# Seven quadrant products for the first mlp's upper projections in the third and fourth batch

## The chip, the cores and the metric

One core of a Trainium2 chip runs the whole program as one launch. The metric is the device time of that launch in microseconds (us); lower is better. The engines are TensorE (PE in the profile; PEld is its weight load), VectorE (DVE), ScalarE (ACT), GpSimd (POOL) and SyncE (SP), which issues most DMAs.

## The reference

Local attention over 4 batches, 8 heads, 576 positions and a head size of 64 gives x with 2304 tokens and 512 features. A first mlp follows: three upper projections from 512 to 768 features, the largest of the three, and a projection back to 512. A second mlp with 8 experts of 1024 hidden features, weighted by gates that are normalised in 8 rounds, gives the output. All numbers are float32.

```python
attn = softmax(mask(q @ k.T / 8)) @ v                      # window of 32, plain or with a step of 4
h = np.maximum(np.maximum(x @ w1, x @ w2), x @ w3)         # first mlp: 512 -> 768, three times
x2 = h @ w_out                                             # 768 -> 512
out = sum(P[:, e:e + 1] * (np.maximum(x2 @ v1[e], 0) @ v2[e]) for e in range(8))
```

## The kernel before

**Precision.** A float32 operand is held as a rounded high part and a low part (its remainder). `split` (L66 to L69) makes both: a copy on ACT for the high part, then a subtraction on POOL or DVE for the low part. A product of two operands takes three matmuls, high by high, high by low and low by high (`PASS`).

**Stages.** The first mlp runs batch by batch in the order of `WORK`: for batch b the six pieces `b.0` to `b.5` (128 hidden features each) through `up`, and then `b.out` through `down`, which projects back to 512 features, stores x2 and feeds the gates. Batch 0 and batch 1 share their last two pieces' weights, so `1.4` and `1.5` stand beside `0.4` and `0.5`. After batch 3 the second mlp begins with its stages (L802 and L756), in which seven products of quadrants already take the place of eight.

**Up.** For each piece, `up` takes the two halves of 288 tokens, and for each half the three projections. A projection is 12 matmuls (4 slices of the 512 features by 3 passes) of 128x128 weights and 288 columns (L377) into one of four PSUM banks of the pool `ps_g`. The first result is copied out by ACT (L383), the second and third are taken into the maximum by DVE (L385), and the last is split by ACT and DVE. The weights of a batch come from `wm1f` in DRAM by `load_w1`, 512 KB for two weight tiles, and are split again by ACT and POOL in every batch.

**Units and hooks.** PE runs in the order in which the program is written; the other engines' orders are made by a planner that simulates the program and prefers what was written earlier among what it takes to be ready. `up` counts a unit after each projection (12 matmuls), `down` after each 288-column result. After each unit `hooks` adds the attention of the next batch by the lists `BEGIN` and `STAGES`: scores and softmax at a head pair's first unit, the transposes 8 and 9 units later, the product with v and the write of x's high and low part (L256, L260) 11 units later. Batch 2's attention begins in batch 0 and runs beside batch 1; batch 3's runs beside batch 2; beside batch 3 there is none. In batches 1 to 3 a softmax is nine ACT instructions with a sum each (L200).

**Early.** Before the last `down`, `early` fetches the first two weight stages and the first 768 tokens of the second mlp, makes the sums T1 to T4 of x2's quadrants on DVE (L598) and splits them into tiles of the pool `xs`, which takes the place of batch 2's x (`xta`) from piece `3.0` on. The planner is free to run it as soon as its data and buffers are there.

**Buffers.** `raw` has 4 tiles, `wa` 8, `cx` 3 (x2 of a batch, the tokens and sums of `early`, and some others). A tile that is asked for takes any buffer that is free by then.

## Time and profile before

| what | value |
|---|---|
| time, median of 3 runs | 1901.99 us (1899.49 to 1902.62) |
| the profiled execution's own time | 1905.52 us |
| its span | 1903.7 us |
| mean granted TensorE clock | 0.99 |
| PE busy / DVE / ACT / POOL | 98% / 68% / 51% / 35% |
| DMA | 435 MB, 229 GB/s over the span |

The page gives busy time, the chain of work that ended last, and groups of instructions. A stretch of the span can be asked for by itself: batch 1 from `1.0` runs from 175.8 to 247.1 us (its `down` from 224), batch 2 from 247.1 to 342.3 us (its `down` from 317.1), batch 3 from 342.3 to 422.5 us (its `down` from 401.8), each bound read off PE's timeline.

### The profile page before, as it was taken

To read this page: it belongs to the slowest core of one execution; us is meant where nothing else is said; L and a number is where in the kernel's file an instruction comes from. 1 tells how busy PE (TensorE), PEld (TensorE's weight loads), DVE (VectorE), ACT (ScalarE), POOL (GpSimd) and SP (SyncE) were. 2 spreads that over 40 slices of the span, in tenths; PEclk is the share of its full clock that TensorE was granted. 3 is DMA by queue.
4 is the path that set the end of the run, shared out by engine and by line. 5 is a ranking of instruction groups with operands and counts; after the bars stand their busy time and mean duration, and the time that the engine had idled before them with its cause. 6 is when DMAs were issued, how large, how long until landed. Compare 5 with 4: busy or idle time off the path is not lost.

```text
span 1903.7 us, 33958 instructions
## 1 busy us (share of the span) xinstructions
PE 1858.2 (98%) x12105; PEld 1751.4 (92%) x12105; DVE 1295.0 (68%) x2454; ACT 966.6 (51%) x2337; POOL 667.2 (35%) x568
## 2 busy tenths in 40 slices
PE   7899999999999999999999999999999999999998
PEld 6799999998899987999899999999989999999997
DVE  7983333437866677666677777777777677876777
ACT  5663544324554444444456454565545554555544
POOL 2123433435666667666612121121211121221211
PEclk7899999999999999999999999999999999999999
DMA  7744444346667668666986766767798676776763
GB/s 257 269 154 168 154 145 166 131 171 232 230 249 260 254 252 307 250 252 257 347 282 223 239 217 226 247 224 237 228 333 265 213 233 225 228 255 212 233 221 100
DMA packets 206537, 435.23 MB, mean 229 GB/s; under 512 B 18848, under 2 KB 97312, under 8 KB 204832
## 3 DMA queue, kind: packets, MB, share of 16 engines
q1 hardware_dynamic: 203680, 429.12, 65.6%
q10 hardware_dynamic: 2688, 3.93, 0.7%
q8 instruction: 96, 1.57, 0.3%
q14 instruction: 73, 0.60, 0.1%
HBM read 313.97 MB, written 119.01 MB: 227 GB/s over the span
## 4 chain that ended last, share of the span: by engine, by line
PE 84%; DVE 8%; DMA 4%; issue 2%; ACT 2%; POOL 1%; SPq 0%; DVEq 0%; ACTq 0%; POOLq 0%
PE po L1011 25%; PE po L1106 12%; PE ps L377 10%; PE po L756 10%; PE p L1106 6%; PE q L1106 6%; PE q L802 4%; PE p L802 4%; PE ps L397 3%; DMA raw<-in_wm 1%; DVE sums L534 1%; DVE h L854 1%; DMA cx<-in_wm 1%; DVE ts L573 1%; DMA qt<-in_q 1%
## 5 line engine op out<-in xcount | busy, mean ns | idle before, releaser
L1011 PE MATMUL po<-wt,hop 128*128 128x256 f32 (+1 forms) x3264 | 482.9, 310 | 2.5 <-DVE r L987 2.5
L1011 PEld LDWEIGHTS po<-wt,hop 128*128 128x128 f32 x3264 | 445.0, 191 | 38.2 <-ACT hop L68 2.7
L69 POOL TENSOR_TENSOR wt<-raw,wt 128x256 fp32r<-128x256 f32 x192 | 186.4, 996 | 757.9 <-ACT wt L68 757.5
L69 DVE TENSOR_TENSOR hop<-r,hop 128x384 fp32r<-128x384 f32 x384 | 208.5, 572 | 190.2 <-ACT hop L68 185.1
L756 PE MATMUL po<-wb,h 128*128 128x512 f32 x1152 | 295.1, 392 | 0.4 <-POOL wb L69 0.4
L377 PE MATMUL ps<-xt,wa 128*128 128x288 f32 x1728 | 244.1, 299 | 5.6 <-DVE wa L290 2.0
L756 PEld LDWEIGHTS po<-wb,h 128*128 128x128 f32 x1152 | 213.5, 188 | 34.2 <-POOL wb L69 1.1
L377 PEld LDWEIGHTS ps<-xt,wa 128*128 128x128 f32 x1728 | 233.6, 190 | 9.6 <-DVE wa L290 2.3
L68 ACT CAST hop<-r 128x384 fp32r<-128x384 f32 x384 | 188.7, 516 | 56.7 <-DVE r L987 30.5
L69 POOL TENSOR_TENSOR wa<-raw,wa 128x512 fp32r<-128x512 f32 x112 | 135.9, 1217 | 89.6 <-ACT wa L68 87.7
L1120 ACT ACTIVATE r<-r 128x384 f32<-128x384 f32 x192 | 99.7, 525 | 127.6 <-DVE r L1119 126.7
L1106 PE MATMUL po<-xT,wa 128*128 128x384 f32 x768 | 155.9, 338 | 0.0
L1106 PEld LDWEIGHTS po<-xT,wa 128*128 128x128 f32 x768 | 136.6, 188 | 0.0
L69 POOL TENSOR_TENSOR tw<-ts,tw 128x512 fp32r<-128x512 f32 x64 | 85.3, 1355 | 93.4 <-DVE h L854 53.7
L1106 PE MATMUL po<-xB,wa 128*128 128x384 f32 x576 | 117.0, 338 | 0.0
L1040 DVE SCALAR_TENSOR_TENSOR acc<-po,prob,acc 128x256 f32<-128x256 f32 x222 | 95.0, 475 | 21.7 <-PE po L1011 17.6
L69 POOL TENSOR_TENSOR wa<-sums,wa 128x512 fp32r<-128x512 f32 x64 | 88.7, 1406 | 55.6 <-ACT wa L68 36.7
L1106 PEld LDWEIGHTS po<-xB,wa 128*128 128x128 f32 x576 | 102.4, 188 | 0.3 <-issue 0.3
L69 POOL TENSOR_TENSOR wb<-raw,wb 128x512 fp32r<-128x512 f32 x64 | 93.0, 1453 | 24.4 <-ACT wb L68 23.9
L981 DVE TENSOR_TENSOR r<-r,r 128x384 f32<-128x384 f32 x128 | 93.1, 727 | 2.2
L1022 ACT COPY mm<-po 128x256 f32<-128x256 f32 x144 | 49.6, 376 | 79.7 <-PE po L1011 79.7
L68 ACT CAST wa<-raw 128x512 fp32r<-128x512 f32 x112 | 61.6, 555 | 56.0 <-DMA raw<-in_wm 29.3
(183 smaller groups left out, 3106.6 us busy)
## 6 DMA issues: line engine op xcount, KB each, us to landing
wa<-wsd SPq DMA_DIRECT2D x192, 512.0 KB, 4.4
wt<-wtd SPq DMA_DIRECT2D x256, 256.0 KB, 3.6
wsd<-wa SPq DMA_DIRECT2D x96, 512.0 KB, 3.4
raw<-in_wm SPq DMA_DIRECT2D x64, 512.0 KB, 4.2
wtd<-tw SPq DMA_DIRECT2D x128, 256.0 KB, 2.8
raw<-in_wm SPq DMA_DIRECT2D x128, 256.0 KB, 5.4
wa<-wsd SPq DMA_DIRECT2D x64, 256.0 KB, 4.5
cx<-in_wm SPq DMA_DIRECT2D x12, 1024.0 KB, 6.9
```

The source lines that it names most:

```text
L68: nc.scalar.copy(hi, src)
L69: sub.tensor_tensor(out=lo, in0=src, in1=hi.bitcast(F32), op=ALU.subtract)
L377: nc.tensor.matmul(ps, w[:, wi, kk], xt[:, xi, kk, n0:n0 + HB], start=(n == 0), stop=(n == 3 * KT - 1),)
L397: nc.tensor.matmul(ps, wo[f][:, wi, d2 * P:(d2 + 1) * P], hs[f][:, hi, a * HB:(a + 1) * HB], start=(f == 0 and n == 0), stop=(f == NF1 - 1 ...
L756: nc.tensor.matmul(po, self.hs[f, j][:, hi, t * P:(t + 1) * P], self.ws[f][:, wi], start=(n + f + k == 0), stop=(n == NPAIR - 1 and f == 1 ...
L802: nc.tensor.matmul(ps, wo[w][:, wi, kk], xo[x][:, xi, kk], start=(first and k == 0), stop=True if k == 5 else False, skip_group_check=not ...
L981: nc.vector.tensor_tensor(out=r[o, n], in0=r[x, n], in1=r[y, n], op=op)
L1011: nc.tensor.matmul(self.ps[side, t][:, 0:x.shape[-1]], h[:, hi, t * P:(t + 1) * P], x, start=(first and i == 0), stop=(n == NPAIR - 1 and ...
L1022: nc.scalar.copy(m, self.ps[ORD[k][0], t][:, 0:256])
L1040: nc.vector.scalar_tensor_tensor(out=a, in0=src, scalar=g, in1=a, op0=ALU.mult, op1=ALU.add)
L1106: nc.tensor.matmul(ps[k][side], wo[k][w][:, wi, kk], xo[x][:, xi, kk], start=(first and c == 0), stop=c == 5, skip_group_check=not first,)
L1120: nc.scalar.activation(out=r, in_=r, func=AF.Relu)
```

## The change

In batches 2 and 3 `up` is replaced by `up_quads`. It takes two pieces at once (256 hidden features) and both halves of the tokens, cuts the weights into quadrants A11 to A22 and x into B11 to B22, and makes the four result quadrants from seven products of quadrants (A11 B11, A12 B21, S2 T2, S1 T1, S3 T3, S4 B22, A22 T4) instead of eight. A product is 6 matmuls of the same shape (2 slices by 3 passes), so a projection of two pieces takes 42 matmuls where it took 48. S2, S3 and A22 add onto the bank `p` of A11 after it has been copied out, S4 onto the bank `q` of S1.

- The weight sums S1 to S4 are made once: nine calls of `sums_w1`, three units apart from unit 58 on (pieces `1.0` to `1.out`), each with two loads, four DVE operations, two splits by ACT and POOL, and two stores of 512 KB into a new DRAM tensor `wsf`. `load_quads` loads them in batches 2 and 3, one projection ahead, beside A11, A12 and A22, which it splits as before.
- Attention's result for batches 2 and 3 is copied whole (`whole`, into a `cx` tile) instead of being split. `quads_first` and `quads_rest` make T1 to T4 on DVE and split all seven operands with ACT and DVE, at units 72 and 85 for batch 2 and 124 and 128 for batch 3.
- The running maximum of a projection over w1, w2, w3 is kept in a `cx` tile, `best`, which lives as long as `up_quads` of its batch. Three of the four results need an addition on DVE before the maximum.
- The two x buffers (`spaces`) now stay allocated to the end. T1, T2 and T3 of the second mlp lie in the first of them, and are loaded in two DMAs each instead of one.

A unit of `up_quads` ends after A12, S1, S4 and A22, so that a batch still has 36 units in `up`, and `BEGIN` is unchanged. The diff, shortened:

```diff
 BEGIN = {1: (0, 5, 10, 16), 2: (43, 60, 67, 73), 3: (92, 100, 108, 116)}
+SUMS = 58
+QUAD = {2: (72, 85), 3: (124, 128)}
...
+SPACE = 2 * KT * S
+QUADS = (("B11", "B21", "T2", "T1"), ("T3", "B22", "T4"))
...
-    xts = {}
+    xts, xf, spaces = {}, {}, [xta_p.tile([P, SPACE], F32R, name="xt")]
...
-        if p == 0:
-            xts[b] = (xtb_p if b % 2 else xta_p).tile([P, 2, KT, S], F32R, name="xt")
-        xt = xts[b]
+        if p == 0 and b < 2:
+            xts[b] = spaces[b].rearrange("p (s k n) -> p s k n", s=2, k=KT)
+        xt = xts.get(b)
...
+        def whole(a):
+            if b not in xf:
+                xf[b] = cx_p.tile([P, KT, S], F32, name="xf", tag="cx")
+            t0, t1 = halves[a]
+            for s0, s1, dst in pieces(t0 * QT, t1 * QT, dil):
+                nc.scalar.copy(dst(xf[b][:, p]), h["o", a][:, s0 - t0 * QT:s1 - t0 * QT])
...
-            ops[f"V{a}"], ops[f"H{a}"], ops[f"L{a}"] = partial(v, a), partial(hi, a), partial(lo, a)
+            ops[f"V{a}"] = partial(v, a)
+            ops[f"H{a}"], ops[f"L{a}"] = (partial(hi, a), partial(lo, a)) if b < 2 else (partial(whole, a), list)
...
+    wsf = dram.tile([3 * NF1 // 2, 2, P, 2, 512], F32, name="wsf")
+    def sums_w1(i):
+        raw = raw_p.tile([P, 2, 512], F32, name="raw")
+        for j in range(2):
+            g = 3 * (2 * (i // 3) + j) + i % 3
+            nc.sync.dma_start(raw[:, j], wm1f[g // 2, :, g % 2])
+        a11, a12, a21, a22 = (raw[:, j, c:c + 256] for j in range(2) for c in (0, 256))
+        for o, x, y, op in (
+            (a22, a21, a22, ALU.add), (a21, a11, a21, ALU.subtract),
+            (a11, a22, a11, ALU.subtract), (a12, a12, a11, ALU.subtract),
+        ):
+            nc.vector.tensor_tensor(out=o, in0=x, in1=y, op=op)
+        for j in range(2):
+            t = wa_p.tile([P, 2, 512], F32R, name="wa")
+            split(nc, t[:, 0], t[:, 1], raw[:, j], nc.gpsimd)
+            nc.sync.dma_start(wsf[i, j], t.bitcast(F32))
+    quads_w, best = {}, {}
+    def load_quads(b, i):
+        if i == 3 * NF1 // 2:
+            return
+        raw = raw_p.tile([P, 2, 512], F32, name="raw")
+        for j, c in ((0, 0), (1, 256)):
+            g = 3 * (2 * (i // 3) + j) + i % 3
+            nc.sync.dma_start(raw[:, j, c:512], wm1f[g // 2, :, g % 2, c:512])
+        a, x, y, z = (wa_p.tile([P, 2, 512], F32R, name="wa") for _ in range(4))
+        split(nc, a[:, 0], a[:, 1], raw[:, 0], nc.gpsimd)
+        nc.sync.dma_start(x.bitcast(F32), wsf[i, 0])
+        nc.sync.dma_start(y.bitcast(F32), wsf[i, 1])
+        split(nc, z[:, 0, 0:256], z[:, 1, 0:256], raw[:, 1, 256:512], nc.gpsimd)
+        quads_w[b, i] = {
+            name: t[:, :, c:c + 256].rearrange("p s (k m) -> p s k m", k=2)
+            for name, t, c in (
+                ("A11", a, 0), ("A12", a, 256), ("S2", x, 0), ("S4", x, 256),
+                ("S3", y, 0), ("S1", y, 256), ("A22", z, 0),
+            )
+        }
+    quads_x = {}
+    def quad(name):
+        k = int(name not in QUADS[0])
+        n = 4 * HB
+        i = QUADS[k].index(name) * n
+        return spaces[k][:, i:i + n].rearrange("p (s k n) -> p s k n", s=2, k=2)
+    def quads_first(b):
+        x = xf[b]
+        b11, b12 = x[:, 0:2, 0:HB], x[:, 0:2, HB:S]
+        src = {"B11": b11, "T1": b11}
+        for name in src:
+            if name == "T1":
+                nc.vector.tensor_tensor(out=b11, in0=b12, in1=b11, op=ALU.subtract)
+            t = quads_x[b, name] = quad(name)
+            split(nc, t[:, 0], t[:, 1], src[name], nc.vector)
+    def quads_rest(b):
+        x = xf.pop(b)
+        b11, b12, b21, b22 = (x[:, k:k + 2, n:n + HB] for k in (0, 2) for n in (0, HB))
+        for name, o, y, z in (
+            ("B21", b21, None, None), ("T2", b11, b22, b11), ("T3", b12, b22, b12),
+            ("B22", b22, None, None), ("T4", b21, b21, b11),
+        ):
+            if y is not None:
+                nc.vector.tensor_tensor(out=o, in0=y, in1=z, op=ALU.subtract)
+            t = quads_x[b, name] = quad(name)
+            split(nc, t[:, 0], t[:, 1], o, nc.vector)
+    def up_quads(b, f, unit):
+        h = [h1_p.tile([P, 2, S], F32R, name="h1") for _ in range(2)]
+        inner[b][f], inner[b][f + 1] = h
+        if f == 0:
+            best[b] = cx_p.tile([P, 2, 2, HB], F32, name="best", tag="cx")
+        for m in range(3):
+            i = 3 * f // 2 + m
+            load_quads(b, i + 1)
+            ws = quads_w.pop((b, i))
+            m1, u2, m5 = (at2_p.tile([P, HB], F32, name="tmp", bufs=3) for _ in range(3))
+            def bank():
+                return ps_g.tile([P, 512], F32, name="ps")[:, :HB]
+            def product(ps, w, x, first):
+                x = quads_x[b, x]
+                n = 0
+                for kk in range(2):
+                    for wi, xi in PASS:
+                        nc.tensor.matmul(
+                            ps, ws[w][:, wi, kk], x[:, xi, kk], start=(first and n == 0),
+                            stop=n == 5, skip_group_check=not first,
+                        )
+                        n += 1
+            def result(j, a, ps, c):
+                hi, lo = (h[j][:, s, a * HB:(a + 1) * HB] for s in range(2))
+                t = best[b][:, j, a]
+                if m == 0:
+                    if c is None:
+                        nc.scalar.copy(t, ps)
+                    else:
+                        nc.vector.tensor_tensor(out=t, in0=ps, in1=c, op=ALU.add)
+                    return
+                if c is None:
+                    c = ps
+                else:
+                    nc.vector.tensor_tensor(out=c, in0=ps, in1=c, op=ALU.add)
+                nc.vector.tensor_tensor(out=t if m == 1 else c, in0=c, in1=t, op=ALU.max)
+                if m == 2:
+                    split(nc, hi, lo, c, nc.vector)
+            p, q = bank(), bank()
+            product(p, "A11", "B11", True)
+            nc.scalar.copy(m1, p)
+            product(q, "A12", "B21", True)
+            result(0, 0, q, m1)
+            hooks(unit)
+            product(p, "S2", "T2", False)
+            nc.scalar.copy(u2, p)
+            q = bank()
+            product(q, "S1", "T1", True)
+            nc.scalar.copy(m5, q)
+            hooks(unit + 1)
+            product(p, "S3", "T3", False)
+            result(1, 1, p, m5)
+            product(q, "S4", "B22", False)
+            result(0, 1, q, u2)
+            hooks(unit + 2)
+            product(p, "A22", "T4", False)
+            result(1, 0, p, None)
+            hooks(unit + 3)
+            unit += 4
...
+    spaces.append(xtb_p.tile([P, SPACE], F32R, name="xt"))
...
+    def tile_x(name):
+        if name not in ("T1", "T2", "T3"):
+            return xs_p.tile([P, 2, 2, HT], F32R, name=f"x{name}")
+        n = 4 * HT
+        i = (int(name[1]) - 1) * n
+        return spaces[0][:, i:i + n].rearrange("p (s k n) -> p s k n", s=2, k=2)
...
-        t = xs_p.tile([P, 2, 2, HT], F32R, name=f"x{name}")
+        t = tile_x(name)
...
     def load_x(blk, name, queue=nc.sync):
-        t = xs_p.tile([P, 2, 2, HT], F32R, name=f"x{name}")
-        x_ops[blk][name] = t
+        t = x_ops[blk][name] = tile_x(name)
         if name[0] == "T":
-            queue.dma_start(t.bitcast(F32), x2t[int(name[1]) - 1])
+            for s in range(2):
+                queue.dma_start(t[:, s].bitcast(F32), x2t[int(name[1]) - 1, :, s])
...
+        if 0 <= unit - SUMS < 27 and (unit - SUMS) % 3 == 0:
+            sums_w1((unit - SUMS) // 3)
+        for b in (2, 3):
+            if unit == QUAD[b][0]:
+                quads_first(b)
+            if unit == QUAD[b][1]:
+                quads_rest(b)
+                load_quads(b, 0)
...
         if what == "3.0":
             at_p.release()
-            xta_p.release()
...
         if f == "out":
             if b == B - 1:
                 early()
             down(b, unit)
+        elif b >= 2:
+            if int(f) % 2 == 0:
+                up_quads(b, int(f), unit)
         else:
             up(b, int(f), unit)
```

## Rows read from the trace of the kernel before

**Rows 1.** The page, parts 1 and 4: busy time by engine; chain by engine.

```profile
PE 1858.2 (98%) x12105; PEld 1751.4 (92%) x12105; DVE 1295.0 (68%) x2454; ACT 966.6 (51%) x2337; POOL 667.2 (35%) x568
PE 84%; DVE 8%; DMA 4%; issue 2%; ACT 2%; POOL 1%; SPq 0%; DVEq 0%; ACTq 0%; POOLq 0%
```

**Rows 2.** Four stretches: length, each engine's busy us, clock, DMA share, GB/s.

```profile
175.80:224.00 48.20, 47.39 (x495) 45.82 (x495) 19.65 (x46) 27.16 (x98) 20.28 (x16) 1.00 0.42 143
247.10:317.10 70.00, 70.00 (x723) 68.06 (x722) 28.38 (x65) 37.71 (x133) 29.15 (x23) 1.00 0.37 124
342.30:401.80 59.50, 58.52 (x441) 58.11 (x441) 28.68 (x49) 22.82 (x49) 27.86 (x21) 1.00 0.28 105
401.80:422.50 20.70, 20.70 (x158) 20.70 (x157) 4.16 (x10) 3.85 (x9) 6.36 (x9) 1.00 0.53 192
```

**Rows 3.** Timeline of PE: start us, length us, operation, xcount, [idle before].

```profile
239.17 1.27 PE L243 MATMUL pso<-pt,vt 96*64 96x64 f32 x36
247.11 4.96 PE L377 MATMUL ps<-xt,wa 128*128 128x288 f32 x36
355.64 46.36 PE L377 MATMUL ps<-xt,wa 128*128 128x288 f32 x348 [0.98 <-DVE h L69]
```

**Rows 4.** Groups by form, 247.1 to 317.1: xcount, busy us, mean ns, idle.

```profile
L385 DVE TENSOR_TENSOR tmp<-ps,tmp 128x288 f32<-128x288 f32 x12 | 5.5, 455 | 14.6 <-PE ps L377 14.6
L383 ACT COPY tmp<-ps 128x288 f32<-128x288 f32 x12 | 4.8, 398 | 6.4 <-PE ps L377 6.4
L230 ACT COPY pt<-pst 96x384 f32<-96x384 f32 x9 | 4.1, 475 | 5.7 <-PE pst L226 5.7
L68 ACT CAST wa<-raw 128x512 fp32r<-128x512 f32 x17 | 10.5, 621 | 9.9 <-PE ps L377 7.9 <-issue 2.1
L69 POOL TENSOR_TENSOR wa<-raw,wa 128x512 fp32r<-128x512 f32 x17 | 21.8, 1290 | 24.8 <-ACT wa L68 24.7
```

**Rows 5.** Timeline of ACT around one softmax of the third batch.

```profile
259.49 0.37 ACT L200 ACTIVATE sm<-sm,st 128x96 f32<-128x96 f32 x1
263.02 0.38 ACT L383 COPY tmp<-ps 128x288 f32<-128x288 f32 x1
```

**Rows 6.** Timeline of the first seven-product stage of the second mlp.

```profile
422.53 1.21 PE L802 MATMUL p<-xB,wa 128*128 128x384 f32 x6
423.59 1.22 PE L802 MATMUL q<-xB,wa 128*128 128x384 f32 x6
423.78 0.48 ACT L868 COPY m<-p 128x384 f32<-128x384 f32 x1 [0.35 <-PE p L802]
424.91 0.56 DVE L859 TENSOR_TENSOR m<-q,m 128x384 f32<-128x384 f32 x1 [1.98 <-PE q L802]
```

**Rows 7.** Timeline of DVE and POOL in the fourth batch.

```profile
346.15 0.95 DVE L598 TENSOR_TENSOR xd<-xh 128x768 f32<-128x768 f32 x1
348.04 1.85 POOL L69 TENSOR_TENSOR xT<-xd,xT 128x768 fp32r<-128x768 f32 x1 [2.07 <-ACT xT L68]
348.37 2.34 DVE L598 TENSOR_TENSOR xd<-xh 128x768 f32<-128x768 f32 x1
```

**Rows 8.** Instructions by line over the whole span, the sums of L534.

```profile
L534 DVE TENSOR_TENSOR sums<-raw 128x256 f32<-128x256 f32 x64 | 42.1, 661 | 69.5 <-DMA raw<-in_wm 69.2 <-POOL wa L69 0.2
```

**Rows 9.** Timeline of DVE, one such sum with POOL idle.

```profile
370.05 0.42 DVE L534 TENSOR_TENSOR sums<-sums,raw 128x256 f32<-128x256 f32 x1
```

**Rows 10.** Two more stretches, columns as in the second group.

```profile
181.00:235.00 54.00, 53.19 (x541) 51.60 (x541) 21.12 (x49) 29.68 (x104) 22.09 (x18) 1.00 0.42 143
905.00:952.00 47.00, 46.63 (x237) 42.30 (x236) 29.09 (x40) 21.50 (x44) 30.77 (x22) 1.00 0.97 346
```

**Rows 11.** Timeline of ACT, five strided copies out of PSUM.

```profile
310.77 1.22 ACT L256 CAST xt<-pso 128x144 fp32r<-128x144 f32 x5
```

**Rows 12.** Timeline of POOL and PE in the fourth batch's down.

```profile
407.01 1.62 POOL L69 TENSOR_TENSOR xg<-x,xg 128x288 fp32r<-128x288 f32 x2 [3.70 <-ACT xg L68]
410.59 0.43 PE L440 MATMUL pg<-xg,wgs 128*128 128x288 f32 x2
```

More of the change, by code (lines that the diff above doesn't have):

```diff
@@ L1171, in attention_moe @@
     fixed.close()
-    for p in (ps_c, ps_o, *reversed(pools), xs_p):
+    for p in (ps_c, ps_o, *reversed(pools), xs_p, xta_p):
         p.release()
```

## Prediction

> **What bounds the kernel now.** I read the page first: PE is busy 98% of the span and carries 84% of the chain that ended last; no other engine passes 68% [rows 1]. Then busy time by stretch. Batch 2's `up` is 70.00 us with PE busy all of it, batch 3's 59.5 us with 58.52, and the other engines stand at 28 to 38 us there [rows 2]. So a matmul less is time less, as long as nothing else gets to be late. The price of one is read off an undisturbed piece of PE's timeline: 348 matmuls of 288 columns in 46.36 us, 133 ns each [rows 3].
>
> Why does nothing wait today? In `up` a result must leave its bank only before the bank is used again, and with four banks PE runs about three results (3 x 1.6 us) ahead of ACT and DVE. A softmax holds ACT for nine instructions on end, from 259.49 to the next copy out of PSUM at 263.02, over 3.2 us [rows 5], and PE doesn't stop. That slack is what the change spends.
>
> **What the change removes.** 9 projections x 6 matmuls x 2 batches = 108 matmuls, 108 x 0.133 = **14.4 us**. All of it lies on PE's path. Also, `early` ran its sums in batch 3 on DVE and cost PE 0.98 us there [rows 3]; those sums need a third `cx` buffer, which `best` now holds, and the place of T1 to T3 in x's own buffer, so they move to the end of `3.5`: **-1.0 us** (bounds 0 and -1.0).
>
> **Batch 3's `up`, the chain of one projection.** S2 adds onto the bank that m1 is copied from, S3 onto u2's, S4 onto m5's, and A22 onto the bank that DVE adds m5 to. Each has one product of other work as cover: 6 x 133 = 0.80 us. The nearest rows are the second mlp's first stage, the same order with 384 columns: products start 1.06 us apart, a product's modelled end is 1.21 us after its start, ACT begins 0.04 us after that end, DVE 0.10 [rows 6]. With 288 columns I estimate a product's end at 0.96 us after its start; ACT's copy (0.40) is then done at 1.41 and DVE's addition (0.46) at 1.52 [rows 4], and the next product on that bank starts at 1.60. So it fits, with 0.1 to 0.2 us to spare for ACT and less than 0.1 for DVE. Those two engines have about 42 and 63 operations of 0.4 us per batch here, 17 and 26 us of some 52. I take **+0.3 us**; the bounds are 0 and 3.6 (each of 36 DVE windows 0.1 us short).
>
> **Batch 2's `up`, with attention between.** Here ACT's run of exponentials meets those short windows. Counted from the end of a pair's scores: the mask and maximum on DVE take 2.3 us, then ACT is held to 5.55. S2, S1, S3, S4 and A22 need 4.0 us and find their copies made; A11 and A12 of the next projection run to 5.6; its S2 needs m1, which stands behind what piled up on ACT at about 0.3 us each (A22's split; after a w1 projection one more copy, after a w3 projection three high parts), so 0.65 us late after w2, 0.95 after w1, 1.5 after w3. The four pairs begin in a w2, w1, w3 and w2 projection: 0.65 + 0.95 + 1.5 + 0.65 = **+3.7 us**. From below 0, if the planner sets the copies between the exponentials. From above each pair costs its whole run and its three transposes' copies, 3.2 + 3 x 0.47 = 4.6 us [rows 4, 5], 18.4 in all. I take the count, since the units of `BEGIN` lie four apart and so each run starts behind A12.
>
> Weights: a projection loads 0.39 MB of A and 1.05 MB of sums where two pieces loaded 0.52; 9 x 1.44 = 13.0 MB against 4.7 per batch. That adds 120 to 160 GB/s to 124 and 105 [rows 2], under the 346 that the trace sustains at a DMA share of 0.97 [rows 10]. The loads are asked for a projection (over 5.6 us) ahead: no charge. SP issues four DMAs a projection for one, and what stands behind them (the next pair's q, k and v) is due many units later. ACT and POOL split 1.5 tiles instead of 2.
>
> **Batch 1, where the sums are made.** Nine calls between 181 and 235 us. DVE: 36 operations x 0.66 [rows 8] = 24 us beside 21.1 [rows 10], together 45 of 54. POOL: 18 x 1.29 [rows 4] = 23 beside 22.1, also 45. ACT: 18 x 0.62 = 11 beside 29.7. DMA: 9 x (0.52 in, 1.05 out) = 14.2 MB beside 143 GB/s x 54 us = 7.7. None is past its stretch by these rows, all are near it. A call puts 2.6 us on DVE ahead of the maxima that free PE's banks; PE's lead is 4.8 us, less what the mask and maximum of a softmax take in the same queue. **+3.0 us**, a third of a microsecond a call; from 0 to the two rivals below.
>
> What a sum costs beside POOL is seen in the fourth batch: 0.95 us with POOL idle, 2.34 when it starts at 348.37 beside a POOL subtraction that ends at 349.89, that is, 0.82 us after the end [rows 7]; a weight sum takes 0.42 with POOL idle [rows 9]. The Trainium skill (SBUF — State Buffer, "SBUF: two separate sides") says that a DVE operation with two SBUF inputs and a GpSimd operation that reads SBUF lock one port pair in turn, and that the later one blocks for the whole of the other. By that rule, which those rows bear out, the sums here could take far more than 0.66 us, as POOL is taken for 45 of 54 us; that is the third rival.
>
> **The two joints.** Between the end of batch 2's last product with v (240.44) and the first matmul of `2.0` (247.11) lie 6.7 us [rows 3]. In it ACT copies five strided pieces, 1.2 us [rows 11], and DVE makes eight operations of 576 columns, 5.9 us in series at an estimated 0.74 (between 0.46 for 288 columns and 0.95 for 768 [rows 4, 7]); B21 is due 7.5 us after that end and ready at about 2.8, T4 due at 12 and ready at 8. They fit when POOL stays away. The same holds before `3.0`, with 4 units of `down` as cover. **+1.0 us** for both (0 to 4).
>
> **The last `down`.** `early` now does there what it did in batch 3: four DVE sums (0.95 to 2.3 us each), four splits, and most of eight weight splits on POOL, where 6.4 us stood in 20.7 [rows 2]. x2's buffer comes free after the sums, and its low parts queue behind POOL's 2 us splits; before, the first of them was made at 407.01 and used by PE at 410.59 [rows 12], 3.5 us of slack against a delay of 4 to 8. **+2.0 us** (0 to 5). The second mlp's stages change by one more DMA issue per T: nothing.
>
> **Sum.** -14.4 - 1.0 + 0.3 + 3.7 + 3.0 + 1.0 + 2.0 = **-5.4 us**. The sum is made against the profiled execution, 1905.5 us (span 1903.7), which gives 1900.1; that execution was 3.5 us above the median of the runs, so for the median 1902.0 I predict **1896.6**.
>
> **Rivals.**
> 1. *All covers hold.* The planner knows the new windows and sets copies ahead of exponentials. For: PE had no idle time in batch 2 [rows 2]. Against: the runs of exponentials are unbroken now [rows 5]. -15.4: 1886.6. Chance 0.14.
> 2. *Batch 1 becomes bound by transfers.* 21.9 MB in 54 us are 405 GB/s; at 346 [rows 10] they take 63 us, 9 us more. If PE waits for all of it (weights behind stores in SP's queue), 9.2 stands in place of 3.0: 1902.8, no change. For: stores hold `wa` tiles that weights need. Against: attention's loads are asked for long ahead. The Trainium skill (DMA: Bandwidth & Descriptors, Specifications) puts a core's share of HBM at 358 GB/s, near the row; by it the stretch would want 61 us. Chance 0.24, with mixtures that end there.
> 3. *Slower: DVE and POOL take turns in batch 1.* If each sum stands behind a POOL operation, 0.42 + 1.29 = 1.7 us each, DVE wants 21 + 62 us in 54. It decides from a mean of 0.91 us (36 x 0.91 = 33 us fill the stretch); each 0.1 us beyond is 3.6 us. At 1.3 us, 14 in place of 3.0: 1907.6. Chance 0.12.
> 4. *Slower: softmax stops PE.* At 18.4 in place of 3.7: 1911.3; it decides from 3.2 us a pair. For: copies are later in the program than the exponentials. Against: the count above. Chance 0.10.
>
> The forecast itself has 0.40. A measurement of this kernel tells about 0.2%, 3.8 us, from no change. Faster by more: 0.40 + 0.14 = 0.54; within: 0.24; slower: 0.22. The range runs from rival 1's time to between rivals 3 and 4: **1887 to 1909**.
>
> **What would show it.** Right: 756 matmuls from `up_quads` at 133 ns; the stretch of batch 2's `up` at 70.0 - 7.2 + 3.7 = 66.5 us, with PE waiting for ACT's m1 copy behind L200; batch 3's at 59.5 - 7.2 - 0.7 = 51.6; batch 1 some 3 us longer; the last `down` 2 us longer, PE waiting for POOL's low parts of x2. Wrong: PE waiting for DVE in every projection (windows too short), for loads of the stored sums, or stretches of the second mlp that differ.

## The result: 0.9% slower, and the profile after

The changed kernel takes 1918.8 us (median, 1915.5 to 1921.2) against 1901.7 for the kernel before on the same chip: a ratio of 1.009, 95% interval 1.0071 to 1.011. The forecast was 1896.6 with a range to 1909, so the sign and the range were both wrong. The profiled execution's span is 1918.7, 15.0 more than before.

The first answer is on the page. Busy time by engine, then the chain that ended last by engine, after (before: [rows 1]):

```profile
PE 1855.9 (97%) x11997; PEld 1745.1 (91%) x11997; DVE 1351.3 (70%) x2538; ACT 995.7 (52%) x2405; POOL 684.8 (36%) x586
PE 78%; DVE 10%; DMA 5%; ACT 3%; issue 2%; POOL 2%; SPq 0%; DVEq 0%; POOLq 0%; ACTq 0%
```

The 108 matmuls are gone (12105 to 11997), yet PE is busy only 2.3 us less: 14.4 us of matmuls went, and PE's share of the chain fell from 84% to 78%. The other matmuls took longer: the 495 of up 1 are busy 50.85 us, where before they were 47.39 [rows 2]. Where the time went, the stretches say. Each bound is the start of the first matmul of a stage on PE's timeline; "0.out" is the first batch's `down`, "up 1" the four pieces `1.0` to `1.3`, and E the start of the second mlp. The two joints of the prediction lie at the ends of 1.out and 2.out.

| kernel | 0.out | up 1 | 1.out | up 2 | 2.out | up 3 | 3.out | E starts |
|---|---|---|---|---|---|---|---|---|
| before | 23.1 | 48.3 | 23.1 | 70.0 | 25.2 | 59.5 | 20.7 | 422.5 |
| after | 29.7 | 59.5 | 23.1 | 69.3 | 23.6 | 54.1 | 26.7 | 437.6 |

E starts 15.1 us later and the span is 15.0 longer: nothing behind the first mlp matters. Batches 2 and 3 give back 6.1 us in their `up` and 1.6 in 2.out; 0.out and up 1, where the sums are made, take 17.7, and the last `down` 6.0. (0.out starts 0.9 earlier.) Five stretches of after, columns as in [rows 2]: bounds, length, busy us of PE, PEld, DVE, ACT and POOL with their instructions, granted clock, DMA share, GB/s:

```profile
151.70:181.40 29.70, 25.13 (x204) 23.91 (x203) 12.04 (x24) 12.96 (x38) 18.75 (x17) 0.97 0.84 299
181.40:240.80 59.40, 50.85 (x495) 48.11 (x495) 30.87 (x58) 31.86 (x108) 31.28 (x24) 0.96 0.77 268
263.90:333.20 69.30, 65.64 (x668) 61.56 (x667) 43.49 (x85) 44.39 (x154) 27.07 (x23) 1.00 0.75 248
356.80:410.90 54.10, 52.57 (x387) 51.47 (x387) 31.24 (x66) 27.52 (x65) 24.26 (x22) 1.00 0.83 293
410.90:437.60 26.70, 23.07 (x159) 22.40 (x158) 14.60 (x21) 7.33 (x15) 13.25 (x11) 0.94 0.41 150
```

The second line is the one to learn from. Up 1 has 495 matmuls, as many as before, and takes 59.4 us; DVE, ACT and POOL are each busy for about 31 of them, DMA for 0.77. **Nothing is full, and PE stands still for 8.5 us.** So the answer isn't in busy shares but in who waits for whom. PE's waits from 150 to 440 us of after, the six largest of ten rows (waiting line, what it waited for, us in total, times, longest):

```profile
PE pst L231 <- ACT pt L235: 5.9, 2, 3.3
PE pg L591 <- POOL xg L74: 5.4, 7, 1.6
PE pg L591 <- ACT xg L73: 3.3, 3, 1.4
PE ps L496 <- DVE tmp L515: 2.0, 2, 1.2
PE ps L496 <- ACT tmp L522: 1.7, 3, 1.0
PE ps L390 <- DVE h L74: 1.5, 1, 1.5
```

In the kernel before, PE's only such wait between 150 and 247 us was 0.8 us. None of these rows names a sum: the waits are for ordinary work (a transpose's copy, a low part of x2 for the gates, a low part of h). For two of them the timeline shows that a part of `sums_w1` stands ahead of it (start, us, engine, line, operation, [idle before it, and what ended that]):

```profile
199.03 0.38 ACT L73 CAST h<-ps 128x288 fp32r<-128x288 f32 x1
201.69 0.43 DVE L417 TENSOR_TENSOR raw<-raw 128x256 f32<-128x256 f32 x1 [5.75 <-DMA raw<-wm1f]
202.61 0.40 DVE L74 TENSOR_TENSOR h<-ps,h 128x288 fp32r<-128x288 f32 x1
203.06 1.85 PE L390 MATMUL ps<-xt,wa 128*128 128x288 f32 x12 [1.47 <-DVE h L74]
...
213.62 0.62 ACT L73 CAST wa<-raw 128x512 fp32r<-128x512 f32 x1 [2.44 <-DMA wsf<-wa]
214.14 0.85 ACT L235 COPY pt<-pst 96x384 f32<-96x384 f32 x2
214.66 0.53 PE L231 MATMUL pst<-ident,sm 128*96 128x128 f32 x3 [2.62 <-ACT pt L235]
```

First: the high part of h is out of its bank at 199.41, but DVE's next instruction is a sum (L417) that sits idle for 5.75 us until its weights land; the low part of h, which PE needs before the bank is free, comes after it, and PE stops. Second: ACT waits 2.44 us for a buffer of `wa` that a store is still emptying; the copy of a transpose stands behind that, and PE stops for 2.62. DVE and ACT count as idle in both.

A stop can cost twice. Two windows of 10 us behind and beside such waits, columns as above:

```profile
180.00:190.00 10.00, 9.05 (x57) 8.59 (x57) 4.36 (x8) 3.58 (x9) 4.57 (x5) 0.86 0.85 308
230.00:240.00 10.00, 7.20 (x69) 6.98 (x70) 1.35 (x5) 6.28 (x26) 3.68 (x4) 0.83 0.99 366
```

The granted clock is 1.00 in all the stretches of [rows 2] (of its two levels, the higher one, 2.4 GHz) and here partly the lower one (1.2 GHz): 24 matmuls that take 3.42 us at 219.51 take 4.95 at 233.08, right after a wait of 3.25. Not every stop does this: behind the wait of 2.62 at 214.66 they took 3.43. From the mean clocks of 0.out and up 1 (0.97 and 0.96 in the lines above) an estimate of the clock's part is 29.7 x 0.03 + 59.4 x 0.04 = 3.3 of the 17.7 us.

### The profile page after: what moved, and what is told of

Same layout as the page of the kernel before. It is cut to its first block, busy times and chain, and to the rows that moved or that the text cites. A ratio compares the mean times of both kernels' runs of the same rounds, so it can differ in the third digit from the quotient of the medians.

```text
span 1918.7 us, 34188 instructions
## 1 busy us (share of the span) xinstructions
PE 1855.9 (97%) x11997; PEld 1745.1 (91%) x11997; DVE 1351.3 (70%) x2538; ACT 995.7 (52%) x2405; POOL 684.8 (36%) x586
## 4 chain that ended last, share of the span: by engine, by line
PE 78%; DVE 10%; DMA 5%; ACT 3%; issue 2%; POOL 2%; SPq 0%; DVEq 0%; POOLq 0%; ACTq 0%
PE po L1180 24%; PE po L1275 12%; PE po L925 10%; PE p L1275 6%; PE q L1275 6%; PE ps L496 4%; PE q L971 4%; PE p L971 4%; PE ps L390 2%; PE ps L548 2%; DMA raw<-in_wm 1%; DMA x2s<-xg 1%; DVE sums L686 1%; DVE h L1023 1%; DVE ts L725 1%
## 5 line engine op out<-in xcount | busy, mean ns | idle before, releaser
L74 POOL TENSOR_TENSOR wa<-raw,wa 128x512 fp32r<-128x512 f32 (+1 forms) x130 | 150.9, 1166 | 112.9 <-ACT wa L73 106.9
L390 PE MATMUL ps<-xt,wa 128*128 128x288 f32 x864 | 128.8, 307 | 4.9 <-DVE h L74 1.8
L390 PEld LDWEIGHTS ps<-xt,wa 128*128 128x128 f32 x864 | 121.5, 197 | 8.1 <-DVE h L74 2.2
L1275 PE MATMUL po<-xt,wa 128*128 128x384 f32 x576 | 116.9, 338 | 0.0
L496 PE MATMUL ps<-xt,wa 128*128 128x288 f32 x756 | 107.9, 299 | 5.2 <-DVE tmp L515 2.0
L496 PEld LDWEIGHTS ps<-xt,wa 128*128 128x128 f32 x756 | 102.0, 188 | 8.9 <-ACT tmp L522 2.8
L73 ACT CAST wa<-raw 128x512 fp32r<-128x512 f32 (+1 forms) x130 | 68.5, 534 | 75.4 <-DMA raw<-in_wm 34.4
L74 POOL TENSOR_TENSOR wa<-sums,wa 128x512 fp32r<-128x512 f32 x64 | 89.2, 1415 | 48.7 <-ACT wa L73 31.0
L1275 PEld LDWEIGHTS po<-xt,wa 128*128 128x128 f32 x576 | 102.5, 188 | 0.0
```

What stands on the lines that cost most here:

```text
L73: nc.scalar.copy(hi, src)
L74: sub.tensor_tensor(out=lo, in0=src, in1=hi.bitcast(F32), op=ALU.subtract)
L390: nc.tensor.matmul(ps, w[:, wi, kk], xt[:, xi, kk, n0:n0 + HB], start=(n == 0), stop=(n == 3 * KT - 1),)
L496: nc.tensor.matmul(ps, ws[w][:, wi, kk], x[:, xi, kk], start=(first and n == 0), stop=n == 5, skip_group_check=not first,)
L1275: nc.tensor.matmul(ps[k][side], wo[k][w][:, wi, kk], xo[x][:, xi, kk], start=(first and c == 0), stop=c == 5, skip_group_check=not first,)
```

## The experiments

One table for all of them; ratios are to the kernel before on the same chip, stretches as above, each of one profiled execution. Three waits of PE in batch 0's last pieces, where sums or splits ran too, stand in none of these stretches: 0.7 us in e8, 1.0 in e11, 3.2 in e15.

| kernel | ratio (95%) | 0.out | up 1 | up 2 | up 3 | 3.out | E starts |
|---|---|---|---|---|---|---|---|
| e1_no_sums | 0.9982 (0.9972 to 0.9991) | 23.1 | 48.7 | 68.0 | 54.6 | 27.7 | 419.2 |
| e2_no_store | 1.0054 (1.0037 to 1.0071) | 29.5 | 56.7 | 68.0 | 54.7 | 27.6 | 433.0 |
| e3_store_only | 1.0002 (0.9992 to 1.0011) | 25.6 | 49.8 | 68.3 | 54.6 | 25.1 | 419.4 |
| e7_dve_only | 1.0018 (1.0007 to 1.0028) | 29.1 | 48.6 | 68.0 | 54.8 | 26.5 | 422.4 |
| e8_split_only | 1.0009 (1.0000 to 1.0019) | 23.1 | 51.9 | 68.1 | 54.8 | 25.1 | 419.9 |
| e11_sums_no_load | 1.0020 (1.0010 to 1.0030) | 26.9 | 48.7 | 68.3 | 54.8 | 25.1 | 422.9 |
| e9_low_on_dve | 1.0095 (1.0080 to 1.0110) | 29.2 | 63.1 | 68.1 | 54.8 | 25.1 | 438.0 |
| e10_before_sums | 1.0080 (1.0059 to 1.0101) | 29.3 | 55.2 | 70.0 | 61.0 | 21.1 | 438.7 |
| e14_paced | 1.0180 (1.0158 to 1.0201) | 23.0 | 78.5 | 69.1 | 54.7 | 26.5 | 455.2 |
| e15_spread | 1.0113 (1.0094 to 1.0132) | 24.7 | 59.3 | 75.4 | 54.8 | 26.6 | 440.8 |
| e13_unsplit | 1.0090 (1.0073 to 1.0108) | 29.7 | 50.3 | 77.2 | 58.1 | 26.6 | 440.6 |
| e4_best_space | 1.0070 (1.0051 to 1.0089) | 29.4 | 59.4 | 69.0 | 59.6 | 21.9 | 436.2 |
| e12_T_loaded | 1.0045 (1.0029 to 1.0060) | 30.6 | 58.1 | 68.9 | 54.4 | 21.0 | 431.7 |
| e5_unfused | 1.0059 (1.0042 to 1.0076) | 28.5 | 58.7 | 67.5 | 56.1 | 26.7 | 433.4 |

**Is it the sums?** In e1_no_sums `sums_w1` isn't called and batches 2 and 3 load stored weights in place of the sums.

```diff
-        if 0 <= unit - SUMS < 27 and (unit - SUMS) % 3 == 0:
-            sums_w1((unit - SUMS) // 3)
...
-        nc.sync.dma_start(x.bitcast(F32), wsf[i, 0])
-        nc.sync.dma_start(y.bitcast(F32), wsf[i, 1])
+        nc.sync.dma_start(x.bitcast(F32), wm1f[i])
+        nc.sync.dma_start(y.bitcast(F32), wm1f[(i + 1) % NG])
```

> Leaves out the making and storing of the weight sums; S1 to S4 are loaded from other stored weights of the same size, so every later instruction and transfer stays. If the 6.5 us lost in batch 0's down (29.7 us where 23.2 stood) and the 11.2 us lost in pieces 1.0 to 1.3 (59.4 where 48.2 stood) belong to the sums, those stretches go back to about 23.5 and 48.5 us and the time falls by 16 to 18 us, to about 1901. If the loss came from the attention copies, the buffers of x or the seven products, it stays above 1912.

0.out and up 1 come back to 71.8 us (before 71.4, after 89.1). The sums are the whole loss there. But even with free sums the change brings 0.2% only.

And e10_before_sums adds `sums_w1` and its calls, unused, to the kernel before.

> The kernel before, with eight products everywhere, and only the making and storing of the weight sums added (nothing reads them). If the sums cost what they cost in the change, this is 15 to 19 us slower than before, about 1918, with batch 0's down near 29 us and pieces 1.0 to 1.3 near 58. If they cost so much only beside the other new work of batch 1 (whole copies of attention, making the x operands), it is under 10 us slower.

Sums alone cost 0.8%, with eight products as well: no meeting with the new projections is needed. Of the 16.2 us by which E starts later, 13.1 lie in 0.out and up 1; up 1 is 55.2, where the expectation had 58.

**Which part of them?** e2_no_store drops the two stores (the sums are made, and other weights loaded).

> Makes the sums and their splits on DVE, ACT and POOL as the change does, but leaves out the stores to DRAM (S1 to S4 come from other stored weights). Theory of stores: the weight tiles are held until slow stores land, ACT's splits wait for them at the head of ACT's queue, and PE stands behind; then this falls to within 4 us of the kernel without sums, 1902 to 1905. Rival, engine time: 36 sums on DVE and 18 subtractions on POOL that shut each other out are the cost; then it stays at 1912 or more, with DVE's mean for a sum unchanged at about 0.69 us.

0.out and up 1 stay at 86.2 us of 89.1: transfers are the small part. e3_store_only drops the sums and splits, and stores the raw tiles instead.

```diff
-        a11, a12, a21, a22 = (raw[:, j, c:c + 256] for j in range(2) for c in (0, 256))
-        for o, x, y, op in (
...
         for j in range(2):
-            t = wa_p.tile([P, 2, 512], F32R, name="wa")
-            split(nc, t[:, 0], t[:, 1], raw[:, j], nc.gpsimd)
-            nc.sync.dma_start(wsf[i, j], t.bitcast(F32))
+            nc.sync.dma_start(wsf[i, j], raw)
```

> Makes only the transfers of the sums: nine calls of two loads and two stores of 512 KB, the stored values being the loaded weights, with no work on DVE, ACT or POOL and no tile of the pool wa. If crowded transfers alone cost the time (x2's stores landing late in batch 0's down), batch 0's down stays at 28 us or more and the time at 1910 or more. If the held weight tiles or the engines' queues are what counts, it falls to 1901 to 1905.

Then e7_dve_only keeps loads and sums without splits and stores, and e8_split_only loads and splits without sums and stores (both load other weights in batches 2 and 3, as e1).

> Makes the 36 sums on DVE and leaves out their splits and stores (S1 to S4 come from other stored weights). Without the stores but with all engine work the time was 1915.6, without any of it 1901.6. If the sums on DVE hold up PE, this stays at 1910 or more, with pieces 1.0 to 1.3 at 54 us or more. If the splits on ACT and POOL do it, it falls to 1902 to 1905.

> Makes the 18 splits on ACT and POOL, of the plain weights, and leaves out the sums on DVE and the stores. If the splits stand ahead of attention's copies on ACT and of x2's low parts on POOL and so stop PE, batch 0's down stays at 28 us or more and the time at 1910 or more. If DVE's sums do it, it falls to 1902 to 1905. If only both together do it, both this and the kernel with sums alone come out near 1904.

Both came out near 1904 (1905.5 and 1904.2 us), the case that e8's expectation names for a loss that only both together bring. Over e1's 71.8 us in 0.out and up 1: transfers 3.6, sums 5.9, splits 3.2 (3.9 with the wait ahead of 0.out), sums with splits 14.4, all 17.3. Alone they add to 12.7. Sums and splits cost 14.4 together and 9.1 apart (9.8 with that wait), so about a third of their price comes only where both are there.

That this is because each stands in line for the other is argued from the timelines, and the sizes have limits. The parts alone stand elsewhere: in e7 the last sum starts at 178.5 us, as up 1 begins; in e2, with the splits, at 212.5. Some of each price is the clock's: by the mean clocks (0.94 in both stretches of e2, 0.94 in e7's 0.out, 0.97 in e8's up 1) an estimate is 5.2, 1.7 and 1.6 us, which leaves 9.2 together against 5.8 apart. And the ratios, over all executions, give 0.72% together against 0.36 + 0.27 = 0.63% apart, which is no difference beyond their intervals.

**Is DVE waiting for late loads?** e11_sums_no_load makes 36 sums of data that are there (the mask and earlier sums), without loads, splits and stores; other weights in batches 2 and 3.

```diff
-        for j in range(2):
-            g = 3 * (2 * (i // 3) + j) + i % 3
-            nc.sync.dma_start(raw[:, j], wm1f[g // 2, :, g % 2])
         a11, a12, a21, a22 = (raw[:, j, c:c + 256] for j in range(2) for c in (0, 256))
+        m1, m2 = mk[:, 0:256], mk[:, 256:512]
         for o, x, y, op in (
-            (a22, a21, a22, ALU.add), (a21, a11, a21, ALU.subtract),
-            (a11, a22, a11, ALU.subtract), (a12, a12, a11, ALU.subtract),
+            (a22, m1, m2, ALU.add), (a21, m1, a22, ALU.subtract),
+            (a11, a22, a21, ALU.subtract), (a12, a21, a11, ALU.subtract),
```

> The 36 sums on DVE of tiles that are already on the chip: leaves out their loads, splits and stores (S1 to S4 come from other stored weights). With loads they cost 0.36% over the kernel without sums (1905.5, batch 0's down 29.1 us). If what costs is DVE standing still at a sum whose load is late, with PE's maxima and copies queued behind it, this falls to within 2 us of 1901.6 and batch 0's down to 23 to 24 us. If it is DVE's time for the sums themselves, it stays at 1904 to 1907.

For the sums alone the theory of late loads falls: without loads they still cost 0.38% over e1 (0.36% with them). Up 1 returns to 48.7 because no sum runs there: the 36 stand between 132.6 and 167.5 us. In 0.out they cost 3.8 us, and 1.0 ahead of it; of the 2.1 us less than in e7, some 1.7 are the clock's (0.94 there in 0.out, 1.00 here). A kernel with splits and stores but without late loads wasn't run, so how much of the whole loss the late loads make, as the one at 201.69, stays open.

**Would another engine do?** e9_low_on_dve makes the sums' low parts on DVE and not on POOL.

```diff
-            split(nc, t[:, 0], t[:, 1], raw[:, j], nc.gpsimd)
+            split(nc, t[:, 0], t[:, 1], raw[:, j], nc.vector)
```

> The whole change, with the low parts of the weight sums made on DVE (18 x 0.67 us) instead of POOL (18 x 1.29 us). If POOL's queue ahead of x2's low parts, and the turns that POOL and DVE take at one port, are the main cost, batch 0's down falls to 24 to 26 us and the time to 1908 to 1912. If what counts is work put in front of others on any queue, DVE takes POOL's place and the time stays within 3 us of 1918.8.

Up 1 is 63.1 in place of 59.5: no gain. Nor does POOL's part decide: with 18 operations fewer on POOL, and as many more on DVE, the loss is as large.

**Is it the place?** The first sum of after runs at 137.2 us, in batch 0's last pieces, though written at unit 58, some 48 us later: the planner sets ahead what it takes to be ready. e14_paced takes the raw tiles from h's pool, whose buffers come free only later; e15_spread puts the calls six units apart.

```diff
-        raw = raw_p.tile([P, 2, 512], F32, name="raw")
+        raw = h1_p.tile([P, 2, S], F32, name="hs", tag="h1")[:, :, 0:512]
```

```diff
-        if 0 <= unit - SUMS < 27 and (unit - SUMS) % 3 == 0:
-            sums_w1((unit - SUMS) // 3)
+        if 0 <= unit - SUMS < 54 and (unit - SUMS) % 6 == 0:
+            sums_w1((unit - SUMS) // 6)
```

> The weight sums take their raw tiles from the pool of h, whose buffers come free only with batch 0's down, so that no sum can stand in the queues before that; all else is as in the changed kernel. In its trace the first sums stand before 150 us, in batch 0's last pieces, and batch 0's down is 29.7 us long against 23.1. Theory A (what costs is that sums are set into batch 0's down, where x's low parts and the gates' operands are due): that down falls to about 23 to 24 us, batch 1's first four pieces stay near 59, total 1912 to 1914. Theory B (27 to 54 operations in three full queues cost the same wherever they stand): the 6 us move to batch 1's pieces or to its down, total 1917 to 1920.

> The nine calls stand six units apart in place of three (units 58 to 106 in place of 58 to 82), so that five of them fall beside batch 2; all else is as in the changed kernel. Theory A (what costs is density: sums, splits and stores in a stretch in which attention and the weights' splits already fill the order of the queues): half as many per unit cost less than half, batch 0's down and batch 1 lose 17.7 us to at most 8, batch 2 gains at most 4, total 1907 to 1913. Theory B (each call costs its 2 us wherever it stands): what batch 1 gives back batch 2 loses, total 1917 to 1921; above that if the short windows of the seven products make a sum dearer there than in batch 1, up to 1926.

Both miss the theory of place and density. e14 gets 0.out back to 23.0, as expected, and pays 19 us more in up 1 and 6.7 in 1.out: the pulling ahead had helped. (The edit also takes buffers from h. In the waits from 174 to 282 us no engine waits to write an h; PE's are for weights, 15.0 us from ACT and 7.3 from POOL, and for the gates.) It shows the line most plainly. Timeline of ACT and PE, e14:

```profile
184.50 1.14 ACT L73 CAST wa<-hs 128x512 fp32r<-128x512 f32 x2 [1.51 <-DVE hs L417]
187.77 0.37 ACT L205 ACTIVATE sm<-sm,st 128x96 f32<-128x96 f32 x1 [2.14 <-DVE st L190]
...
191.29 1.14 ACT L73 CAST wa<-hs 128x512 fp32r<-128x512 f32 x2
192.33 1.14 ACT L73 CAST wa<-raw 128x512 fp32r<-128x512 f32 x2
192.99 0.85 PE L390 MATMUL ps<-xt,wa 128*128 128x288 f32 x2 [6.00 <-ACT wa L73]
```

The weights that PE needs now (wa<-raw, 192.33) stand behind a softmax and behind the split of a sum (wa<-hs) that is needed only in batch 2, 90 us later. PE waits 6.00 us here and 5.77 and 3.25 at the next two such places.

In e15 four of the nine calls (the expectation says five, a miscount) are written beside batch 2. The planner evens that out in its own way. The 36 sums by stretch, first of after (0.out, up 1), then of e15 (0.out, up 1, up 2); the rest run before 0.out (a sum that straddles a bound counts in both):

```profile
L417 DVE TENSOR_TENSOR raw<-raw 128x256 f32<-128x256 f32 x11 | 7.5, 684 | 0.9 <-DMA raw<-wm1f 0.7
L417 DVE TENSOR_TENSOR raw<-raw 128x256 f32<-128x256 f32 x16 | 11.2, 700 | 12.0 <-DMA raw<-wm1f 11.9
...
L417 DVE TENSOR_TENSOR raw<-raw 128x256 f32<-128x256 f32 x6 | 2.5, 424 | 1.6 <-DMA raw<-wm1f 1.5
L417 DVE TENSOR_TENSOR raw<-raw 128x256 f32<-128x256 f32 x15 | 10.8, 717 | 8.3 <-DMA raw<-wm1f 6.1 <-POOL wa L74 1.9
L417 DVE TENSOR_TENSOR raw<-raw 128x256 f32<-128x256 f32 x8 | 5.0, 631 | 0.1
```

So up 1 kept 15 of its 16 sums and its 59.3 us; 0.out has 6 for 11 and loses 1.6 us for 6.5; up 2 has 8 and loses 7.4 over e1. In these stretches a sum with its share of splits and stores costs PE 0.3 to 0.9 us (6.5 / 11, 11.2 / 16, 1.6 / 6, 10.6 / 15, 7.4 / 8). Ahead of 0.out the price runs from nothing to several us. The nine or ten sums of after there cost nothing that a row shows: from 120 us to 0.out PE has no wait, as in e1. In e15 seven sums between 137 and 149 us end a softmax's maximum 2.9 us later than in e1, the copy that frees a bank stands behind that softmax on ACT, and PE stops for 3.15 us.

A call costs 2.0 us in after (17.7 / 9), 2.5 in e15 (19.6 and the 3.15, over 9), and 4.1 in e14 (36.5 / 9), where tiles come free late and nothing can be set ahead. Spreading the calls made none cheaper, which is nearer to the other theory, but a call has no fixed price: it goes by what stands behind it. How calls would fare in up 1 at a lower density than 15 sums, neither kernel reached.

**The splits at the use?** e13_unsplit stores the sums unsplit (half the bytes) and splits them in `load_quads`.

```diff
-        for j in range(2):
-            t = wa_p.tile([P, 2, 512], F32R, name="wa")
-            split(nc, t[:, 0], t[:, 1], raw[:, j], nc.gpsimd)
-            nc.sync.dma_start(wsf[i, j], t.bitcast(F32))
+        nc.sync.dma_start(wsf[i], raw)
...
+        s = raw_p.tile([P, 2, 512], F32, name="raw")
+        nc.sync.dma_start(s, wsf[i])
+        split(nc, x[:, 0], x[:, 1], s[:, 0], nc.gpsimd)
+        split(nc, y[:, 0], y[:, 1], s[:, 1], nc.gpsimd)
```

> The weight sums are stored once and unsplit (half the bytes), and split by ACT and POOL at each use in batches 2 and 3; same result. By the parts measured (sums alone 0.36%, splits alone 0.27%, transfers alone 0.20% over none), batch 1's cost falls by about half, 8 to 9 us; two more splits a projection in batches 2 and 3 cost 0 to 6 us there. So 1910 to 1917. If ACT's and POOL's extra splits break the short windows of the seven products, batch 2's up goes over 72 us and the time to 1920 or more.

Up 1 gives 9.2 us back, batches 2 and 3 lose 7.9 and 4.0, at the short windows (PE's waits from 240 to 460, e13):

```profile
PE ps L495 <- ACT tmp L521: 8.9, 7, 2.1
PE ps L495 <- DVE tmp L514: 4.8, 4, 2.5
```

**The last `down`.** e12_T_loaded loads T1 to T4 of the second mlp's first tokens (other data of x2 stands for them) and makes no sums for them.

```diff
-        *_, src = sums_x(fetch_x(0, nc.scalar))
...
-            split_x(x_ops[0], name, src, nc.vector if i % 2 else nc.gpsimd)
+            t = x_ops[0][name] = tile_x(name)
+            for s in range(2):
+                nc.sync.dma_start(t[:, s].bitcast(F32), x2s[:, s, 0:2, 0:HT])
```

> Leaves out the fetch, the sums and the splits that make T1 to T4 of the second mlp's first tokens; the four tiles are filled by DMAs of stored x instead. Everything else is the change. If the last down's extra 6.0 us come from that work standing on DVE and POOL ahead of x2's copies and low parts, the last down falls from 26.7 to 21 to 22 us with batch 3's up still at 54 us, and the time by 5 us to about 1914. If the weight splits of the second mlp or the transfers cause it, the last down stays at 25 us or more.

3.out falls from 26.7 to 21.0: its loss comes with `early`'s fetch, sums and splits, which are left out here. e4_best_space lets `early` run in batch 3 as before, by putting `best` into the spare quarter of the second x buffer (rounded there like a high part).

```diff
-            best[b] = cx_p.tile([P, 2, 2, HB], F32, name="best", tag="cx")
+            best[b] = spaces[1][:, 12 * HB:16 * HB].rearrange("p (j a n) -> p j a n", j=2, a=2)
```

> The running maximum lies in the unused quarter of the second x buffer instead of a cx tile, and is kept rounded there, which leaves out its low part. If the last down lost its 6.0 us (26.7 for 20.7) because the second mlp's sums waited for that cx tile, the sums run inside batch 3's up again, the last down falls to 21 to 23 us, and the time to about 1914. If the wait is for the buffer of T1 to T3, which batch 3 still reads, the last down stays at 25 us or more.

3.out falls by 4.8 and up 3 grows by 5.5, most of it one wait of PE (timeline of DVE and PE, e4):

```profile
406.87 2.58 DVE L74 TENSOR_TENSOR xt<-xh,xt 128x768 fp32r<-128x768 f32 x1
409.37 2.05 DVE L516 TENSOR_TENSOR tmp<-tmp,xt 128x288 f32<-128x288 f32 x1
...
412.14 0.45 DVE L515 TENSOR_TENSOR tmp<-ps,tmp 128x288 f32<-128x288 f32 x1
412.64 1.81 PE L496 MATMUL ps<-xt,wa 128*128 128x288 f32 x6 [4.66 <-DVE tmp L515]
```

A low part of `early`'s T (2.58 us) and a maximum that took 2.05 stand on DVE ahead of the addition (L515) that has a window of 0.8 us. Neither of the two places is free: 4.8 us in the last `down`, or 5.5 beside short windows.

**Softmax in batch 2.** e5_unfused gives the attention that runs beside batch 2 one long exponential in place of nine short ones.

```diff
-b, p, at_p, *load_qk(b, p, at_p), None, True,
+b, p, at_p, *load_qk(b, p, at_p), None, b != 3,
```

> Batch 3's softmax (beside batch 2's up) takes one exponential on ACT over all nine blocks, with the subtraction on POOL and the sum on DVE, instead of nine in a row; the result is the same. If the runs of nine on ACT are what holds up batch 2's up (69.3 us where 62.8 of PE work stands), that stretch falls to 64 to 66 us and the time to about 1915. If the stall there is the sum of all short windows, or DVE's, the stretch stays at 68 us or grows, since DVE and POOL get 1 and 1.6 us a pair more.

Up 2 is 67.5, against 69.3 in the changed kernel and 68.0 to 69.1 in the ten others with the nine exponentials and no further work in batch 2. So the run is worth 0.5 to 1.8 us, far from the fall to 64 to 66 us and close to the other theory's 68. The time, 1915.5 us, is the one that the expectation gave for the larger fall, but not for its reason: of the 4.2 us by which E starts earlier, 1.8 lie in up 2 and 1.9 in 0.out and up 1, which the edit doesn't touch.

## Why the prediction was wrong, step by step

- **Matmuls.** 108 went. Right in number; the 14.4 us could not be kept.
- **Batch 1, +3.0, a third of a microsecond a call.** The step that failed: it is 17.7 us in 0.out and up 1, 2.0 a call. Not for its prices. 36 sums took 0.680 us each, against 0.66 in the working (groups of 130 to 230 us: busy, mean ns | idle before, releaser):

```profile
L417 DVE TENSOR_TENSOR raw<-raw 128x256 f32<-128x256 f32 x36 | 24.4, 680 | 13.0 <-DMA raw<-wm1f 12.5
L73 ACT CAST wa<-raw 128x512 fp32r<-128x512 f32 x31 | 18.2, 620 | 25.6 <-DMA wsf<-wa 17.9 <-issue 3.2 <-PE ps L390 3.0
```

  The inference was wrong: "none is past its stretch by these rows" took busy time that fits for work that hides. The idle columns show what it left out: DVE idle 12.5 us in front of sums for their loads, ACT 17.9 in front of splits (18 of the sums, 13 of other weights) for `wa` buffers under store. In the rows at 201.69 and 213.62 the ordinary work behind such an instruction waits with it. The working charged a call with 2.6 us of DVE against 4.8 of lead; a call in fact puts in line a load, 2.7 us of sums, two splits on ACT, two on POOL and two stores, each waiting for one before it. And it took unit 58 for the place, where the planner began 48 us earlier and took 0.out too, in which x2's low parts for the gates stand in the same queues.
- **The rivals for batch 1.** Transfers (rival 2) cost 3.6 us alone, not 9. DVE and POOL in turn (rival 3) is seen in single sums: the longest, 1.83 us against 0.41, starts at 202.92 beside a POOL operation of 1.63 us from 202.84. But the mean of 0.680 is under the 0.91 from which it was to decide. The rule of the Trainium skill (SBUF — State Buffer, "SBUF: two separate sides") thus agrees with the long one and doesn't account for the loss. The time landed past rival 4's, by a mechanism that none of the four held.
- **Batch 2, 66.5 forecast.** 69.3, and 68.0 without the sums. The windows' price is 68.0 - 62.8 = 5.2 us for 3.7 forecast. The mechanism of the 3.7 is there, but smaller: in e1 two of the four pairs stop PE for ACT's m1 copy (L522), 0.35 and 1.04 us, where the count had 0.65 to 1.5 in each. Ahead of both copies stand a run of nine exponentials and what piled up behind it (timelines of ACT and PE, e1):

```profile
290.96 0.36 ACT L205 ACTIVATE sm<-sm,st 128x96 f32<-128x96 f32 x1
...
291.64 0.40 ACT L73 CAST wa<-raw 128x256 fp32r<-128x256 f32 x1
...
293.15 0.40 ACT L522 COPY tmp<-ps 128x288 f32<-128x288 f32 x1
293.61 5.95 PE L496 MATMUL ps<-xt,wa 128*128 128x288 f32 x42 [1.04 <-ACT tmp L522]
```

  What the forecast put at nothing is the rest: 0.5 us for m5 (L530), 0.7 for DVE (L515) and pauses too short for a row. After has 1.3 us more than e1; 1.0 of it is a wait at 268.50 for the u2 copy (L527), which stands on ACT behind a high part of x2 that waited 1.61 us for a store. (The pairs begin eight units apart, and not four; each still begins behind A12.)
- **Batch 3, 51.6 forecast.** 54.1 (54.6 in e1), so, if `early`'s -1.0 came in full, the short windows took 2.8 us of the 3.6 that stood as their upper bound; 1.5 of it is two waits, 1.2 for DVE (L515) and 0.3 for ACT (L522). Taking 0.3, near the lower end, was the error: 0.1 us of slack, worked out from a 384-column row, is not cover.
- **The joints, +1.0.** No loss there: 1.out is unchanged, 2.out 1.6 us shorter, by what isn't shown. The wait of 1.0 us at 268.50 comes after the joint, in up 2.
- **The last `down`, +2.0.** 6.0. The cause was named rightly (e12); the size left out that three waits add (0.7, 1.4 and 1.5 us) and that the clock can fall with them (0.94 of 26.7 us, an estimate of 1.6). Two of the waits, one for ACT, one for POOL, on PE's timeline after, where [rows 12] had none:

```profile
422.17 0.40 PE L591 MATMUL pg<-xg,wgs 128*128 128x288 f32 x1 [1.40 <-ACT xg L73]
424.12 0.40 PE L591 MATMUL pg<-xg,wgs 128*128 128x288 f32 x1 [1.55 <-POOL xg L74]
```

- **The errors lie mostly on one side.** 14.7 us in batch 1, 2.8 in batch 2's `up`, 2.5 in batch 3's, 4.0 in the last `down` are 24.0 too cheap; against that 2.6 for the joints and 0.9 for the earlier start of 0.out were too dear. 24.0 - 3.5 = 20.5, the step from -5.4 to the measured +15.1.

No version ran faster than before by more than free sums would give (0.9982). Whether a hand-written order of the sums, which fills gaps of the three queues without a wait, could come near that wasn't tried.

## What to carry to other kernels

When PE is busy 98% of the time, work added on the other engines is not priced by whether its busy time fits, but by what each of its instructions may wait for and which of PE's suppliers stands behind it on that queue. A chain over load, DVE, ACT, POOL and store puts a wait into every queue it touches, and parts that cost little alone (3.6, 5.9 and 3.2 us) were 17.3 together. A saving of 0.7% of the matmuls should be weighed against that before its matmuls are counted.

## What the runs showed of the hardware

- The same waits of PE were followed by a lower granted clock in some executions and not in others. Twelve kernels have the same three waits in 3.out (0.7, 1.4 and 1.5 us): in four the clock stays at 1.00 and 3.out takes 25.1 us, in six it is 0.94 and 26.5 to 26.7, in two 0.88 and 27.6 or 27.7. So differences in the column 3.out of up to 2.6 us are the clock's. The first and the last, e8 and e1:

```profile
394.80:419.90 25.10, 21.49 (x158) 20.81 (x157) 14.55 (x21) 7.32 (x15) 13.25 (x11) 1.00 0.44 159
391.50:419.20 27.70, 24.09 (x159) 23.41 (x157) 14.57 (x21) 7.52 (x15) 13.23 (x11) 0.88 0.40 145
```

- Behind 3.25 us of waiting 24 matmuls took 4.95 us at 233.08, behind 2.62 us 3.43, as at full clock. In e14's up 1, with waits of 6 us, the mean clock is 0.80 (173.7 to 252.2):

```profile
173.70:252.20 78.50, 56.15 (x496) 53.10 (x496) 32.99 (x73) 34.45 (x111) 31.36 (x26) 0.80 0.61 212
```

- Transfers of loads and stores together reached 366 GB/s for 10 us (230 to 240 us of after, DMA share 0.99); the Trainium skill (DMA: Bandwidth & Descriptors, Specifications) gives about 358 as the limit of HBM for a core; the measurement is 2% above that.
